# Letting one fill follow another inside a request, and putting the exact heads' outputs behind the exponential

## The chip, the cores and the metric

The kernel runs on one core of one Trainium2 chip. The metric is the device time of one execution in microseconds (us); a run of the comparison gives the median of several executions. TensorE is called PE, VectorE DVE, ScalarE ACT and GpSimd POOL, as in the profile. SyncE (SP) issues nearly all DMAs. PSUM has eight banks of 128 x 512 fp32; here they are one tile, `whole_psum`, cut into views.

## The reference

Three stages follow each other (two batches, eight heads, 576 rows, head size 64; 1152 rows of 512 columns afterwards):

```python
def _attn_ref(q, k, v, tau):
    scores = q @ k.T / sqrt(64)
    thresh = max(scores, -1) - tau
    scores = where(scores >= thresh, scores, -1e9) - max
    attn = exp(scores);  attn = attn / (sum(attn) + 1e-9)
    return attn @ v                              # (2, 8, 576, 64) -> x (1152, 512)

def _moe_ref(x, w_gate, w1, w2):                 # 8 experts, hidden 1024
    P = exp(x @ w_gate - max);  8 times: normalise P over rows, then over columns, times N / E
    return sum_e P[:, e] * (relu(x @ w1[e]) @ w2[e])

def _moe2_ref(x, domain_probs, w1, w2):          # 4 experts
    return sum_e p[:, e] * (relu(x @ w1[e]) @ w2[e])
```

## The kernel before

**Numbers in two parts.** Most matmuls work on fp32r operands, and a value is kept as a high part (a cast by ACT) and a low part (the value less its high part, by POOL or DVE). A product is three matmuls: low times high, high times low, high times high.

**Attention, in steps.** The work is 72 units of 128 query rows. Units 0 to 15 are the first 256 rows of batch 0 (two units for each of eight heads): the *exact heads*, whose probabilities and values are multiplied in fp32 (line 376). Heads 0 and 1 also have fp32 scores (`ws`, line 275), and their exponential has a bias of its own, `st[:, 1:2]`. Units 16 to 35 are the other 320 rows of batch 0 (five units for a pair of heads), units 36 to 71 are batch 1 (nine units for a pair). `Attention.step` is called for t = -2 to 76 and writes out by hand the order in which instructions reach the engines' queues. In step t it handles several units at once: scores of unit t+2 on PE (`scores`), the row maximum of unit t+1 on DVE (`top`, line 287) and its exponential on ACT (`exp`, lines 303 and 305), the mask and row sum of unit t (`mask`, line 309), its reciprocal (`norm`, line 317) and the scaling on POOL (line 319), the five transposes of unit t-2 on PE (`turn`, lines 327 and 329), which have one PSUM bank for all units, their copies out of PSUM (`hi` on ACT, line 341; `lo` on DVE, lines 356 and 358), and the products with V of the head that ended with unit t-3, t-4 or t-5 (`mix`). So the reduction of line 287 with number t+2 belongs to step t.

An exact head's product with V is spread over three steps, so its output comes in step t with unit t-5, in even steps from 6 to 20. `out` puts two things down: on ACT the high part `xh` (line 393), and in a list `later` the low part `xl` on DVE (line 396), which also gives the PSUM bank back. `later` is run in the same step, after the scores of unit t+2. In the order of ACT's queue the output's cast stands ahead of the exponential of unit t+1; the exponential stands ahead of `cook`'s cast of a weight tile (line 107, even steps 0 to 12), whose low part is POOL's (line 109).

**The fill.** Two experts of the first mixture are computed on PE between these steps, by generators (`expert_fill`). Layer 1 is eight hidden tiles of 12 matmuls (line 536), layer 2 one output tile for each 128 rows with 24 matmuls of 512 columns (line 564). A generator yields after four matmuls of layer 1 and after two of layer 2; the yielded number is zero where a tile ends and its bank goes back. `todo` holds four generators with the step after which each may start: expert 0 on rows 0 to 255 (after step 20), expert 0 on rows 256 to 575, expert 1 on rows 0 to 255, expert 1 on rows 256 to 575 (all after step 39). A step calls `fill` twice, ahead of the scores and at the end; both ask `pull(n)` for pieces: three together in a step before step 33, two or one to step 39, four after that, where the second call gets something only with a tile open or with no product with V about. `pull` returns where a tile ends and where a generator ends.

**After the attention** two more generators (expert 1 on batch 1) are put on the list, and a loop runs `pull(3)` until it is empty. The loop's counter n also times the gate (`gate`, from n = 7 on with every third n), the sums of x that the later stages need (`sums`), the scaling of the first two experts (`scale`, lines 933 and 935) and the preparation of weights (`tick`, three times from n = 18). What is left of these goes on in the first part of the next stage.

**The rest**, from 322 us on, are the other experts by a seven-product scheme (lines 1132 and 1444); the diff doesn't touch it.

Of the kernel before, what the change touches and what calls it, by code (L numbers as in the profile page):

```python
# [12 lines left out]
ALU = mybir.AluOpType  # L13
# [14 lines left out]

@with_exitstack
def attention_two_moe_kernel(ctx, tc, qP, kP, qT, kT, vp, tau, wg, w1, w1s, w2, w2s, dp, m2w1s, m2w2, m2w2s, out):  # L30
    nc = tc.nc
    V, A, G, T = nc.vector, nc.scalar, nc.gpsimd, nc.tensor

    def f(ap):
        return ap.bitcast(F32)
# [22 lines left out]
    lin = cp.tile([P, 2], F32, name="lin")  # L58
# [19 lines left out]
    def split(eh, el, hi, lo, src):  # L78
        if eh is A:
            A.copy(hi, src)  # L80
        elif eh is V:
            V.tensor_copy(hi, src)
        else:
            G.tensor_scalar(hi, src, 1.0, 1.0, op0=ALU.mult, op1=ALU.mult)
        el.tensor_tensor(lo, src, f(hi), op=ALU.subtract)  # L85
# [28 lines left out]
    class Expert:  # L114


        def __init__(self, i):
            self.w1 = lambda ft: cooked[2 * FT * i + ft]
            self.w2 = lambda ft: cooked[2 * FT * i + FT + ft]


    class Attention:
# [5 lines left out]
        def __init__(self, pl, ps_s, ps_t, ps_r, ps_m):  # L128
            self.pl, self.ps_s, self.ps_t, self.ps_r, self.ps_m = pl, ps_s, ps_t, ps_r, ps_m
            self.units, self.heads = [], []  # L130
            self.t = -2
            self.work = {}
            self.later, self.late = [], []
            self.iq = self.iv = self.lq = self.lv = 0
            self.xf = {}
            self.e2, self.eth = pl.tile([P, 5, 640], F32, tag="eth", name="e2"), None
            self.e32 = pl.tile([P, 5, 512], F32, tag="etl", name="e32")
            self.etl = None
            self.qz = [pl.tile([P, 3 * D], F32R, name=f"qz{i}") for i in range(2)]
            for z in self.qz:  # L140
                V.tensor_scalar(z[:, D:2 * D], ident[:, :D], 0.0, None, op0=ALU.mult)
# [147 lines left out]
        def line(self, u):  # L289
            st = u["st"]  # L290
            if not u["q"][0][0]["exact"]:
                A.activation(st[:, 2:3], st[:, 0:1], AF.Identity, bias=on[:, 1:2], scale=-1.0)
                return
            if not u["q"][0][0]["ws"]:
                V.tensor_scalar(st[:, 2:3], st[:, 0:1], -1.0, on[:, 0:1], op0=ALU.mult, op1=ALU.subtract)
                return
            V.tensor_scalar(st[:, 1:2], st[:, 0:1], lin[:, 0:1], None, op0=ALU.mult)
            V.tensor_scalar(st[:, 2:3], st[:, 0:1], lin[:, 1:2], None, op0=ALU.subtract)

        def exp(self, u):  # L300
            ex = u["ex"] = self.pl.tile([P, 2, HS], F32, tag="ex", name="ex", bufs=4)
# [85 lines left out]
        def out(self, g):  # L387
            hd, n, pv, pl = g["head"], g["n"], g["pv"], self.pl
            h, t0 = hd["h"], hd["b"] * S + g["q0"]
            r0 = (h % 2) * D  # L390
            r, kt, c = slice(r0, r0 + D), h // 2, slice(t0, t0 + n)
            if hd["exact"]:
                A.copy(xh[r, kt, c], pv[r, :n])

                def low():
                    V.tensor_tensor(xl[r, kt, c], pv[r, :n], f(xh[r, kt, c]), op=ALU.subtract)
                    self.ps_m.give(pv)

                self.later.append(low)
                return  # L400

            key = hd["h"] // 2, g["n"]
            if key not in self.xf:
                self.xf[key] = pl.tile([P, n], F32, tag=f"xf{n}", name="xf", bufs=1)
            xf = self.xf[key]
            o = slice(D - r0, 2 * D - r0)
            A.copy(xf[r, :n], pv[o, :n])

            def rest():
                V.tensor_tensor(xf[r, :n], pv[r, :n], xf[r, :n], op=ALU.add)  # L410
                self.ps_m.give(pv)
                if "half" in self.xf.setdefault(key + ("n",), {}):
                    del self.xf[key], self.xf[key + ("n",)]
                    self.late.append(lambda: split(A, G, xh[:, kt, c], xl[:, kt, c], xf[:, :n]))
                else:
                    self.xf[key + ("n",)]["half"] = True

            self.later.append(rest)
# [5 lines left out]
                w()  # L424

        def flush(self):
            self.run(self.later)
            self.run(self.late)

        def step(self, fill, side):  # L430

            us, t = self.units, self.t
            un = lambda i: us[i] if 0 <= i < len(us) else None
            self.load()
            nxt, a, d, x, c, z, y = (un(t + i) for i in (2, 1, 0, -2, -3, -4, -5))
            if x:
                self.turn(x)
            if d:
                self.mask(d)
            if a:  # L440
                self.top(a)
            if d:
                self.guard(d)
            if a and a["q"][0][0]["exact"]:
                self.line(a)
            if d:
                self.norm(d)
            for part, u in ((2, y), (1, z), (0, c)):
                for g in u["mix"] if u else ():
                    if g["head"]["exact"]:  # L450
                        self.mix(g, part)
            end = t > len(us)
            if x and not end:
                self.hi(x)
            for u, late in ((z, False), (y, True)):
                for g in u["mix"] if u else ():
                    if late == g["head"]["exact"]:
                        self.out(g)
            if end:
                self.run(self.later)  # L460
            if x and end:
                self.hi(x)
            if a:
                self.exp(a)
                if not a["q"][0][0]["exact"]:
                    self.line(a)
            fill(0, bool(c and c["mix"]))
            if x:
                self.lo(x)
            if nxt:  # L470
                self.scores(nxt)
            self.run(self.later)
            for g in c["mix"] if c else ():
                if not g["head"]["exact"]:
                    self.mix(g, 0)
            for w in self.work.pop(t, ()):
                w()
            fill(1, bool(c and c["mix"] or z and z["mix"]))
            self.run(self.late)
            side()  # L480
            self.t += 1
            return self.t < len(us) + 5
# [111 lines left out]
    with ExitStack() as att:  # L594
# [5 lines left out]
        at = Attention(ap, ps_s, ps_t, ps_r, ps)  # L600
# [20 lines left out]
        def side():  # L621
            if at.t >= -1:
                fetch(2)
            if at.t >= nA0 - 3 and raws and room[0] and (at.t % 3 < 2 if at.t < nA1 else room[0] > 2 or at.t % 2):
                room[0] -= 1
                cook()
            if at.t == 20:
                nc.sync.dma_start(wg_sb, wg)
                nc.sync.dma_start(dp_sb, dp)
            if at.t == 24:  # L630
                split(V, V, wg2[:, :, :E1], wg2[:, :, E1:], wg_sb)

        def free(n):
# [4 lines left out]
        todo = [(nA0 + 4, expert_fill(hp, X0, 0, 256, near, acc, None, 0, at.later, keep)),  # L638
                (nA1 + 3, expert_fill(hp, X0, 256, 320, far, acc, tail0[0], 0, at.later, free)),
                (nA1 + 3, expert_fill(hp, X1, 0, 256, near, y1, None, 0, at.later, keep)),  # L640
                (nA1 + 3, expert_fill(hp, X1, 256, 320, far, y1, tail0[1], 0, at.later, keep))]

        left, spent = [0], [0]
        few = dict(zip(range(nA1 - 3, nA1 + 4), (2, 2, 2, 2, 2, 1, 1)))

        def pull(n, end=True):

            for i in range(n):
                if not todo or at.t <= todo[0][0] or (left[0] == 1 and not end):
                    return i  # L650
                left[0] = next(todo[0][1], -1)
                if left[0] < 0:
                    todo.pop(0)
                if left[0] <= 0:
                    left[0] = 0
                    return i + 1
            return n

        def fill(phase, busy):
            if phase == 0:  # L660
                if 0 <= at.t < nA0 - 3 and at.t % 2 == 0:
                    room[0] -= 1
                    cook()
                spent[0] = pull(few.get(at.t, 3))
            elif left[0] or not busy:
                pull(max(few.get(at.t, RA1 if at.t < nA1 + 3 else RA2) - spent[0], 0), True)
# [4 lines left out]
        while left[0]:  # L671
            pull(1)
# [921 lines left out]
```

## Time and profile before

| | us |
|---|---|
| median of 3 runs | 1287.18 (1287.1 to 1287.38) |
| profiled execution, its own time | 1286.37 |
| its span, first to last instruction | 1284.6 |
| PE busy | 1267.8 (99%) |
| POOL, DVE, ACT busy | 897.7 (70%), 880.5 (69%), 736.4 (57%) |

The span is the time from the first to the last instruction; 1.77 us lie around it. An engine's busy time is the union of its instructions. The matmuls' ends are modelled, so a busy PE may still be waiting a little: the distance of two starts is firmer than an idle time. "idle before <- releaser" names the instruction after which an engine could go on.

### The profile page before, as it was taken

The numbers are of one execution on the slowest core, as the hardware profiler recorded it, in microseconds if no ns is written. First come the engines' busy times: TensorE is split into PE (matmuls) and PEld (weight loads), VectorE is DVE, ScalarE is ACT, GpSimd is POOL, SyncE is SP. The second block draws the span as 40 slices with busy tenths as digits, with TensorE's granted clock in tenths as the row PEclk, the third lists the DMA queues.
The fourth block names the chain that finished last, engine by engine and source line by source line (L and its number), as shares of the span: only waits on it lengthen the run. The fifth ranks groups of instructions, "written<-read, shape, count | busy, mean of one in ns | idle before, by whom it ended". The sixth has DMA issues, their size and how long they took to land.

```text
span 1284.6 us, 25109 instructions
## 1 busy us (share of the span) xinstructions
PE 1267.8 (99%) x9373; PEld 1207.6 (94%) x9373; DVE 880.5 (69%) x1851; ACT 736.4 (57%) x1483; POOL 897.7 (70%) x987
## 2 busy tenths in 40 slices
PE   8998999999999999999999999999999999999998
PEld 5597988888889999999999999999989999999998
DVE  6888888666637666666666666666745666666667
ACT  6887887423446555555655555566546465555553
POOL 7997987405796767867776786777668568677770
PEclk9999999999999999999999999999999999999999
DMA  5542330101221112211111221111212012111102
GB/s 171 161 125 78 97 98 17 42 1 34 79 70 51 42 42 58 58 34 51 50 42 42 58 59 34 50 51 42 58 36 61 20 51 58 35 58 50 42 18 74
DMA packets 43225, 73.84 MB, mean 57 GB/s; under 512 B 5216, under 2 KB 12512, under 8 KB 43104
## 3 DMA queue, kind: packets, MB, share of 16 engines
q1 hardware_dynamic: 42816, 71.96, 19.4%
q8 instruction: 74, 1.21, 0.4%
q14 instruction: 47, 0.39, 0.1%
q10 hardware_dynamic: 288, 0.28, 0.1%
HBM read 69.86 MB, written 2.36 MB: 56 GB/s over the span
## 4 chain that ended last, share of the span: by engine, by line
PE 87%; DVE 5%; POOL 3%; issue 2%; ACT 2%; DMA 0%; SPq 0%; DVEq 0%; POOLq 0%; ACTq 0%
PE mm L1132 34%; PE mm L1444 33%; PE mm L564 5%; PE mm L536 5%; PE mm L282 2%; PE mm L1252 2%; PE mm L327 2%; DVE ex L309 1%; PE mm L376 1%; POOL wl L85 1%; DVE st L287 1%; PE mm L385 1%; DVE etl L358 1%; PE mm L383 1%; ACT ex L305 1%
## 5 line engine op out<-in xcount | busy, mean ns | idle before, releaser
L85 POOL TENSOR_TENSOR wl<-raw,wh 128x512 fp32r<-128x512 f32 x217 | 282.9, 1310 | 179.8 <-ACT wh L80 166.6
L1232 DVE SCALAR_TENSOR_TENSOR acc<-mm,p,acc 128x256 f32<-128x256 f32 (+1 forms) x428 | 195.3, 508 | 72.2 <-PE mm L1444 59.3
L1444 PE MATMUL mm<-wh,h 128*128 128x256 f32 x960 | 173.3, 279 | 0.0
L1139 ACT COPY snap<-mm 128x576 f32<-128x576 f32 x126 | 80.9, 642 | 157.1 <-DVE mm L1293 77.9
L80 ACT CAST wh<-raw 128x512 fp32r<-128x512 f32 x217 | 133.5, 627 | 47.3 <-PE mm L1444 26.4
L1444 PEld LDWEIGHTS mm<-wh,h 128*128 128x128 f32 x960 | 146.5, 188 | 0.0
L1132 PE MATMUL mm<-xh,wl 128*128 128x288 f32 x672 | 145.7, 298 | 0.3
L1132 PE MATMUL mm<-xh,wh 128*128 128x288 f32 x672 | 143.3, 294 | 0.0
L1132 PE MATMUL mm<-xl,wh 128*128 128x288 f32 x672 | 143.0, 294 | 0.0
L1444 PE MATMUL mm<-wl,h 128*128 128x256 f32 x480 | 134.5, 280 | 0.1
L1444 PE MATMUL mm<-wh,tails 128*128 128x256 f32 x696 | 126.1, 279 | 0.0
L85 POOL TENSOR_TENSOR wl<-sum,wh 128x512 fp32r<-128x512 f32 x82 | 107.1, 1307 | 8.2 <-ACT wh L80 8.1
L1132 PEld LDWEIGHTS mm<-xh,wl 128*128 128x128 f32 x672 | 106.3, 188 | 3.1 <-DVE mm L1152 0.5
L1132 PE MATMUL mm<-xth,wl 128*128 128x288 f32 x504 | 108.1, 295 | 0.1
L1132 PE MATMUL mm<-xtl,wh 128*128 128x288 f32 x504 | 107.7, 294 | 0.0
L1132 PE MATMUL mm<-xth,wh 128*128 128x288 f32 x504 | 107.5, 294 | 0.0
L1132 PEld LDWEIGHTS mm<-xl,wh 128*128 128x128 f32 x672 | 107.5, 188 | 0.0
L1132 PEld LDWEIGHTS mm<-xh,wh 128*128 128x128 f32 x672 | 107.3, 188 | 0.0
L1444 PEld LDWEIGHTS mm<-wh,tails 128*128 128x128 f32 x696 | 106.2, 188 | 0.0
L80 ACT CAST wh<-sum 128x512 fp32r<-128x512 f32 x82 | 51.5, 628 | 85.4 <-POOL sum L829 71.9
L1444 PE MATMUL mm<-wl,tails 128*128 128x256 f32 x348 | 97.2, 279 | 0.0
L1444 PEld LDWEIGHTS mm<-wl,h 128*128 128x128 f32 x480 | 90.1, 188 | 0.5 <-issue 0.3
(242 smaller groups left out, 3487.8 us busy)
## 6 DMA issues: line engine op xcount, KB each, us to landing
raw<-in_w1s SPq DMA_DIRECT2D x56, 256.0 KB, 2.6
raw<-in_w2s SPq DMA_DIRECT2D x48, 256.0 KB, 2.6
raw<-in_w SPq DMA_DIRECT2D x40, 256.0 KB, 3.2
raw<-in_m2w1s SPq DMA_DIRECT2D x32, 256.0 KB, 2.6
raw<-in_m2w2s SPq DMA_DIRECT2D x28, 256.0 KB, 2.7
kr<-in_kT SPq DMA_DIRECT2D x22, 288.0 KB, 3.0
vr<-in_vp SPq DMA_DIRECT2D x24, 160.0 KB, 2.3
qr<-in_qT SPq DMA_DIRECT2D x8, 288.0 KB, 2.9
```

The lines of the kernel that those rows point to most:

```text
L80: A.copy(hi, src)
L85: el.tensor_tensor(lo, src, f(hi), op=ALU.subtract)
L282: T.matmul(sc[:m, hf, :HS], lhsT=q, rhs=kk[:, hf * HS:(hf + 1) * HS], start=i == 0, stop=i == len(ops) - 1)
L287: V.tensor_reduce(st[:, 0:1], u["sc"][:, :, :HS], axis=AX.XY, op=ALU.max, negate=not u["q"][0][0]["ws"])
L327: T.transpose(et[:, kt], exf[:, kt * P:(kt + 1) * P], ident)
L536: T.matmul(ph[:, :n], lhsT=a[:, kt * P:(kt + 1) * P], rhs=x[:, kt, n0:n0 + n], start=i == 0 and kt == 0, stop=i == 2 and kt == KT - 1)
L564: T.matmul(py, lhsT=x, rhs=a, start=i == 0, stop=i == 3 * FT - 1)
L1132: T.matmul(ch[b][:, g, :HS], lhsT=w[:, (2 * g + kt) * P:(2 * g + kt + 1) * P], rhs=operand(u, kt, lo), start=first and j == 0, stop=j == l ...
L1139: A.copy(v[u], m)
L1232: V.scalar_tensor_tensor(a, src, s, a, op0=ALU.mult, op1=ALU.add)
L1252: T.matmul(py, lhsT=hid[x][:, kk, o:o + P], rhs=w[y], start=n == 0, stop=n == 3 * HF - 1)
L1444: T.matmul(m, lhsT=hid(x, kt + ko), rhs=wk[y], start=first and n == 0, stop=n == 5, skip_group_check=True)
```

## The change

The diff does four things. (1) `pull` goes on with the next generator where one ends, within the same request, instead of returning. (2) In an exact head's output step the exponential of unit t+1 and the cast of a weight come ahead of the output's cast `xh`. (3) The output's low part goes to a list `behind`, which is run in the next step, after the reciprocal and ahead of the products with V. (4) On DVE the bias of heads 0 and 1 is made right after the maximum, and the reciprocal comes ahead of the threshold's instruction (`line`).

```diff
@@ -130,7 +130,7 @@
             self.units, self.heads = [], []
             self.t = -2
             self.work = {}
-            self.later, self.late = [], []
+            self.later, self.late, self.behind = [], [], []
             self.iq = self.iv = self.lq = self.lv = 0
             self.xf = {}
             self.e2, self.eth = pl.tile([P, 5, 640], F32, tag="eth", name="e2"), None
@@ -294,8 +294,11 @@
             if not u["q"][0][0]["ws"]:
                 V.tensor_scalar(st[:, 2:3], st[:, 0:1], -1.0, on[:, 0:1], op0=ALU.mult, op1=ALU.subtract)
                 return
+            V.tensor_scalar(st[:, 2:3], st[:, 0:1], lin[:, 1:2], None, op0=ALU.subtract)
+
+        def bias(self, u):
+            st = u["st"]
             V.tensor_scalar(st[:, 1:2], st[:, 0:1], lin[:, 0:1], None, op0=ALU.mult)
-            V.tensor_scalar(st[:, 2:3], st[:, 0:1], lin[:, 1:2], None, op0=ALU.subtract)
 
         def exp(self, u):
             ex = u["ex"] = self.pl.tile([P, 2, HS], F32, tag="ex", name="ex", bufs=4)
@@ -396,7 +399,7 @@
                     V.tensor_tensor(xl[r, kt, c], pv[r, :n], f(xh[r, kt, c]), op=ALU.subtract)
                     self.ps_m.give(pv)
 
-                self.later.append(low)
+                self.behind.append(low)
                 return
 
             key = hd["h"] // 2, g["n"]
@@ -424,6 +427,7 @@
                 w()
 
         def flush(self):
+            self.run(self.behind)
             self.run(self.later)
             self.run(self.late)
 
@@ -439,12 +443,14 @@
                 self.mask(d)
             if a:
                 self.top(a)
+            if a and a["q"][0][0]["ws"]:
+                self.bias(a)
             if d:
                 self.guard(d)
+                self.norm(d)
             if a and a["q"][0][0]["exact"]:
                 self.line(a)
-            if d:
-                self.norm(d)
+            self.run(self.behind)
             for part, u in ((2, y), (1, z), (0, c)):
                 for g in u["mix"] if u else ():
                     if g["head"]["exact"]:
@@ -452,19 +458,21 @@
             end = t > len(us)
             if x and not end:
                 self.hi(x)
-            for u, late in ((z, False), (y, True)):
-                for g in u["mix"] if u else ():
-                    if late == g["head"]["exact"]:
-                        self.out(g)
+            for g in z["mix"] if z else ():
+                if not g["head"]["exact"]:
+                    self.out(g)
             if end:
                 self.run(self.later)
             if x and end:
                 self.hi(x)
             if a:
                 self.exp(a)
-                if not a["q"][0][0]["exact"]:
-                    self.line(a)
+            if a and not a["q"][0][0]["exact"]:
+                self.line(a)
             fill(0, bool(c and c["mix"]))
+            for g in y["mix"] if y else ():
+                if g["head"]["exact"]:
+                    self.out(g)
             if x:
                 self.lo(x)
             if nxt:
@@ -646,11 +654,14 @@
         def pull(n, end=True):
 
             for i in range(n):
-                if not todo or at.t <= todo[0][0] or (left[0] == 1 and not end):
-                    return i
-                left[0] = next(todo[0][1], -1)
-                if left[0] < 0:
-                    todo.pop(0)
+                left[0] = -1
+                while left[0] < 0:
+                    if not todo or at.t <= todo[0][0]:
+                        left[0] = 0
+                        return i
+                    left[0] = next(todo[0][1], -1)
+                    if left[0] < 0:
+                        todo.pop(0)
                 if left[0] <= 0:
                     left[0] = 0
                     return i + 1
```

## Rows read from the trace of the kernel before

**Rows 1.** The page's head and its first part: busy us (share) and instructions.

```profile
span 1284.6 us, 25109 instructions
...
PE 1267.8 (99%) x9373; PEld 1207.6 (94%) x9373; DVE 880.5 (69%) x1851; ACT 736.4 (57%) x1483; POOL 897.7 (70%) x987
```

**Rows 2.** Windows of PE's stages: us, busy time of each engine (instructions), clock, DMA.

```profile
20.00:60.00 40.00, 39.61 (x213) 24.06 (x211) 32.27 (x102) 34.26 (x68) 37.46 (x43) 1.00 0.51 149
60.00:132.00 72.00, 66.97 (x459) 59.69 (x458) 64.60 (x165) 58.02 (x131) 59.96 (x72) 1.00 0.36 103
132.00:232.00 100.00, 98.40 (x684) 91.45 (x683) 86.64 (x222) 78.69 (x176) 80.38 (x115) 1.00 0.24 68
232.00:322.00 90.00, 90.00 (x544) 79.79 (x543) 54.49 (x150) 26.15 (x65) 31.04 (x78) 1.00 0.08 27
```

**Rows 3.** PE's waits over the span: us in total, times, longest.

```profile
PE mm L327 <- DVE etl L358: 2.7, 6, 0.9
```

**Rows 4.** Line 287: duration min/median/max in ns, first and last start in us.

```profile
L287 DVE TENSOR_REDUCE st<-mm x72: 744/753/758, 6.0 to 227.9; 128x1 f32<-128x576 f32 x72
```

**Rows 5.** Timeline, steps 0 and 1: start, us, engine, line, what [idle before].

```profile
9.37 0.14 DVE L313 TENSOR_SCALAR st<-st 128x1 f32<-128x1 f32 x1
...
9.80 0.83 ACT L303 ACTIVATE ex<-mm,st,esc 128x576 f32<-128x576 f32 x1 [0.47 <-DVE st L297]
```

**Rows 6.** Timeline of ACT and POOL around an exact output (step 8).

```profile
30.15 0.37 ACT L393 CAST xh<-mm 64x256 fp32r<-64x256 f32 x1 [0.67 <-PE mm L376]
30.55 0.74 ACT L305 ACTIVATE ex<-mm,st 128x576 f32<-128x576 f32 x1
...
31.18 0.61 ACT L107 CAST wh<-raw 128x512 fp32r<-128x512 f32 x1
...
31.88 1.27 POOL L109 TENSOR_TENSOR wl<-raw,wh 128x512 fp32r<-128x512 f32 x1 [0.31 <-ACT wh L107]
```

**Rows 7.** POOL's waits from 12 to 44 us.

```profile
POOL wl L109 <- ACT wh L107: 1.6, 4, 0.7
```

**Rows 8.** Timeline, the transposes of step 16.

```profile
49.75 0.66 PE L327 MATMUL mm<-ident,ex 128*128 128x128 f32 x4 [0.18 <-POOL ex L319]
```

**Rows 9.** Timeline of DVE and PE, steps 20 and 21.

```profile
64.45 0.43 DVE L396 TENSOR_TENSOR xl<-mm,xh 64x256 fp32r<-64x256 f32 x1
...
64.93 0.82 DVE L309 SCALAR_TENSOR_TENSOR ex<-mm,st,ex 128x576 f32<-128x576 f32 x1
...
65.07 0.62 PE L536 MATMUL mm<-xl,wh 128*128 128x256 f32 x4
...
66.60 0.67 DVE L358 TENSOR_TENSOR tails<-mm,eth 128x512 fp32r<-128x512 f32 x1
```

**Rows 10.** Timeline, steps 39 and 40.

```profile
126.47 0.27 PE L329 MATMUL mm<-ident,ex 128*64 128x128 f32 x1
...
127.70 0.88 POOL L85 TENSOR_TENSOR xl<-xf,xh 128x320 fp32r<-128x320 f32 x1 [1.94 <-ACT xh L80]
...
127.77 0.53 PE L282 MATMUL mm<-kh,qs 128*128 128x288 f32 x2 [1.03 <-DVE ex L309]
```

**Rows 11.** The chain that ended last, from 128 us: start, us, what.

```profile
130.17 1.76 PE mm L536 x12
```

**Rows 12.** Timeline, steps 55 and 56.

```profile
178.16 0.59 ACT L568 COPY acc<-mm 128x512 f32<-128x512 f32 x1 [1.23 <-PE mm L564]
...
180.11 0.63 PE L327 MATMUL mm<-ident,ex 128*128 128x128 f32 x4 [0.91 <-DVE etl L358]
```

**Rows 13.** Timeline of PE in step 71.

```profile
229.64 0.63 PE L327 MATMUL mm<-ident,ex 128*128 128x128 f32 x4 [0.16 <-DVE etl L358]
```

**Rows 14.** Lines 933 and 935: as rows 4.

```profile
L933 DVE TENSOR_SCALAR acc<-acc,p x9: 479/481/491, 308.6 to 322.8; 128x512 f32<-128x512 f32 x9
...
L935 DVE SCALAR_TENSOR_TENSOR acc<-y,p,acc x4: 750/753/754, 312.5 to 316.1; 128x512 f32<-128x512 f32 x4
```

**Rows 15.** Timeline of DVE at the start of the next stage.

```profile
328.80 0.76 DVE L1141 TENSOR_TENSOR mm<-snap,mm 128x576 f32<-128x576 f32 x1 [3.32 <-PE mm L1132]
```

## The prediction

> **What bounds the kernel now.** Read the page's first part first: PE is busy 1267.8 of 1284.6 us [rows 1]. Then cut the span by stage: from 232 us on PE is full (90.00 of 90), so whatever happens there, its matmuls set the time; from 20 to 60 us it is nearly full (39.61 of 40), from 60 to 132 us it lacks 5.03 us, from 132 to 232 us 1.60 us [rows 2]. So the change can give back only PE's idle time in the attention, and the fill's matmuls are the same before and after: one that runs earlier in a hole shortens the loop behind the attention by its own length, one that runs earlier where PE is full shortens nothing. PE's waits say who makes the holes: mostly the transposes, whose one PSUM bank is emptied late by DVE [rows 3]. Steps are found in the trace by line 287, whose 72 reductions are the steps -1 to 70 [rows 4].
>
> **The handover.** Going through `fill` and `pull` with the counts of the code (units of 2 for an exact head, 5 and 9 for a pair): the first generator's last piece falls in step 39. Before, steps 40, 55 and 70 ask for three pieces and get nothing, since the first request meets a generator's end, and the second call is refused there (no tile open, a product with V about). After, step 40 already does the second generator's first tile, and everything behind comes forward: the third generator begins in step 54 instead of 56, the fourth in 68 instead of 71. In the loop the ends of generators cost nothing any more, and 24 matmuls of layer 2 have gone into the attention: 41 requests instead of 48. Each of the three steps is one hole:
>
> Step 40. PE ends its transposes and waits 1.03 us for the mask before the scores [rows 10]. The new tile is 12 matmuls of 320 columns, 1.76 us [rows 11], and stands just there. But it needs rows 256 to 575 of every head, and the last head's low part is POOL's only from 127.70 to 128.58 [rows 10]. The eighth matmul, the last that multiplies it, can't start before; after it five of 0.147 us remain (1.76 / 12), so the scores start at about 129.3 instead of 127.77. 1.5 to 1.6 us later for 1.76 us of work: a gain of 0.2 us. It is bounded by the whole wait, 1.03, and by -0.3, if DVE's row maximum (which has to wait for these scores) is late by some tenths.
>
> Step 55. PE waits 0.91 us for its next transposes, since ACT copies an output tile out at 178.16 ahead of the copy that empties the transposes' bank [rows 12]. After, that output ends in step 53, and PE has a tile of layer 1 in step 54 and another in 55 to do meanwhile. I take the whole 0.9. The ends are 0 (the wait turns up before another of the fill's tiles) and 0.91.
>
> Step 70. 0.16 us of waiting at the transposes behind it [rows 13]; I take 0.15, between 0 and 0.16.
>
> Sum 1.25, at most 2.1, at least -0.5. On the same three holes the Trainium skill has a rule ("Perfetto Trace Analysis", section "Per-instruction lifecycle: what the profiler-reported window actually captures"): a matmul's end in a profile is computed from its size, not observed, so an idle time behind one is no measurement. By it the hole of step 40 is better taken between starts, 126.47 to 127.77 [rows 10], an upper end of 1.30 instead of 1.03; with that the sum's upper end would be 2.4. No run here shows the end itself; the view's 1.03 is 127.77 less 126.47 less the modelled 0.27.
>
> What comes forward with it: weights of expert 1 are cooked as its predecessor's tiles come free, one of them in step 44 instead of 48 (a cast on ACT and a low part on POOL, 0.61 and 1.27 us as in [rows 6], and SP's fetch for the next); neither engine is full there, and I count nothing for it. In the loop, the gate keeps its beat of three requests and ends at request 39 of 41, not of 48: three scaled tiles (of nine; two of 0.48 + 0.75 us, one of 0.48, together 2.9 us [rows 14]) go behind the loop, into DVE's queue in the next stage. DVE idles 3.32 us there before line 1141 [rows 15], so they are hidden, with little to spare: 0 to 0.3 us, I take 0. PE has no hole in the loop that the missing requests could open (90.00 of 90 [rows 2]).
>
> **The exact heads.** Heads 0 and 1: the exponential waits for its bias, and the bias for `guard`, 0.14 us [rows 5]. The guard goes behind it. PE's scores there wait for the mask, so the first steps gain 0.14 us once (0 to 0.42 over three steps).
>
> Output steps: ACT waits 0.67 us for the product with V, casts the output (0.37 us), and only then starts the exponential, at 30.55; the weight's cast comes after it, and POOL has waited 0.31 us for that [rows 6]; 1.6 us of such waits lie between 12 and 44 us [rows 7]. After, exponential and cast start some 0.5 us earlier. But PE is what is full in these steps: all that it can win from 20 to 60 us is 40 - 39.61 = 0.39 us [rows 2], of which the one place that POOL holds up is 0.18 us [rows 8]. I take 0.2, between 0 and 0.39. The output's cast, now behind the weight's, and its low part, now a step later on DVE, hold only the PSUM bank of that product; the next one but one that needs it comes in the step behind that, after the low part in DVE's and PE's order. On DVE the low part's 0.43 us move from the end of an even step to the middle of an odd one, ahead of the copies that free the transposes' bank; the earlier exponential (0.37 us of cast that it no longer waits for) pays for it. No moved instruction issues a DMA, and SP's queue keeps its order.
>
> The last output is the exception. It comes in step 20, and step 21 begins the fill, whose tile needs rows 0 to 255 of all heads: the eighth matmul multiplies the last head's low part. Before, that is made at 64.45 to 64.88, at the end of step 20, and the four matmuls that use it start at 65.07, and span 0.62 us, so that the eighth starts about 0.35 later, at 65.4 [rows 9]: just in time. After, it stands in step 21 behind mask, maximum, guard and reciprocal. From the mask's start to the next thing behind the reciprocal is 66.60 - 64.93 = 1.67 us [rows 9]. The mask itself can come earlier by about 0.45 us (0.43 of low part and 0.37 of cast are no longer ahead of it), so the low part is there at 64.93 - 0.45 + 1.67 + 0.43 = 66.58 instead of 64.88. PE's fill waits 66.58 - 65.4 = 1.18 us, and behind the waiting matmul stand in PE's queue five more of the tile, the scores of unit 23, a product with V and the next transposes; ACT's copies and its next exponential wait for those. I take 1.1 us. The ends: 0, if PE arrives that much later for other reasons or later holes swallow it, and 1.6, if the mask gains nothing.
>
> Sum for the exact heads: -0.14 - 0.2 + 1.1 = +0.8 us; with -1.25 from the handover, -0.45 us. The profiled execution took 1286.37 us, 1.77 more than its span; less 0.45 that is 1285.92. The median is 0.81 us above this execution, so **1286.7 us** is what I predict for it.
>
> **Rivals.** (a) The handover is worth its holes whole and step 21 costs nothing: PE's later holes (5.03 us to 132 us [rows 2]) take the delay in. For it: most of PE's waits for DVE at the transposes [rows 3] come after step 21; against: DVE waits in its turn for what PE is late with. -0.14 - 0.39 - 2.1 = -2.6: 1284.6 us.
>
> (b) Slower: the wait of the fill in step 21. Its place is the eighth matmul of line 536, its price is the time from 65.4 to the end of the low part, at most 1.6 us (mask not earlier), and it decides as soon as it is more than the handover and the first steps give together. The handover gives nothing if the tile in step 40 waits as reckoned and the hole of step 55 only moves by two steps; then 1287.18 + 1.6 = 1288.8 us. For it: all of the chain that it stands in (low part, matmul, scores, transposes) is visible in one step; against: the exponential's earlier start, which pays part.
>
> (c) The change doesn't do what it says: the three empty steps are filled, but where PE was held by DVE it is held a step later, and step 21 costs what the rest gives: 1287.2 us.
>
> **Chances.** The forecast 0.45, (a) 0.25, (b) 0.15, (c) 0.15. No change is here what a measurement of this kernel can't tell from it, 0.2% or 2.6 us either way: below 1284.6 lie most of (a), 0.2, and 0.05 of the forecast's own spread; above 1289.8 lie half of (b), whose price could add to other new waits, and 0.02 more; so faster 0.25, same 0.65, slower 0.10. The range goes from 1284.1, a little below (a), to 1288.7, all but the end of (b).
>
> **What would show it.** In the trace after: requests for the fill in steps 40, 54, 55 and 70 with PE's wait for the mask in step 40 turned into one for POOL's `xl` inside line 536; no wait of 0.9 us at the transposes near 180 us; the exponential of even steps starting right behind DVE's maximum; the weights' low parts on POOL without waits between 23 and 44 us; PE's wait of about 1.1 us inside the first fill tile near 65 us, released by DVE line 396; PE as full from 232 us on as now. The forecast is wrong if no such wait stands in step 21, if the hole of step 55 is still there under another name, or if the next stage begins with PE waiting for DVE.

## The result, and the profile after

The changed kernel takes 1300.12 us (median of 5 runs, 1299.61 to 1300.39) against 1287.26 us of the kernel before (5 runs, 1287.1 to 1287.4): a ratio of 1.0099, 95% interval 1.0087 to 1.011. It is 12.9 us slower; 1286.7 us was predicted. In the changed kernel's lines the numbers have moved by 3 to 11: 327, 358, 396 and 568 are now 330, 361, 399 and 576; 536, 564, 933 and 1132 are 544, 572, 944 and 1143; line 919 is the gate's matmul, line 916 the last of the DVE instructions in front of it, and line 85 makes low parts everywhere.

The page's head and its first part answer to [rows 1]; PE has 5.4 us more of busy time for the same 9373 matmuls:

```profile
span 1298.4 us, 25098 instructions
...
PE 1273.2 (98%) x9373; PEld 1212.6 (93%) x9373; DVE 883.1 (68%) x1851; ACT 736.2 (57%) x1483; POOL 898.0 (69%) x987
```

The windows by stage (columns as in [rows 2]: us, busy time of each engine, granted clock, DMA) show where:

```profile
20.00:60.00 40.00, 39.73 (x213) 24.21 (x213) 33.32 (x104) 34.61 (x68) 37.81 (x43) 1.00 0.53 150
60.00:132.00 72.00, 66.33 (x451) 58.82 (x450) 62.91 (x158) 56.50 (x127) 58.45 (x74) 1.00 0.37 103
132.00:232.00 100.00, 98.60 (x685) 91.90 (x684) 84.05 (x216) 77.83 (x173) 79.93 (x115) 1.00 0.23 68
...
308.00:312.00 4.00, 0.92 (x6) 0.43 (x4) 2.38 (x10) 1.93 (x5) 4.00 (x10) 1.00 0.35 90
312.00:316.00 4.00, 4.00 (x12) 3.18 (x12) 3.62 (x11) 0.00 (x0) 3.29 (x11) 0.57 0.36 109
316.00:328.00 12.00, 12.00 (x55) 9.84 (x54) 4.17 (x18) 3.69 (x9) 1.31 (x1) 1.00 0.00 0
328.00:332.00 4.00, 2.02 (x15) 1.77 (x13) 3.72 (x7) 1.68 (x3) 0.98 (x1) 1.00 0.26 66
332.00:336.00 4.00, 1.56 (x6) 1.48 (x7) 4.00 (x7) 0.00 (x0) 2.07 (x2) 0.59 0.40 116
336.00:340.00 4.00, 4.00 (x20) 4.00 (x20) 2.92 (x6) 1.16 (x2) 1.39 (x1) 0.56 0.06 19
```

The attention is about as full as before. Behind it, where PE had 90.00 of 90 us, there are two holes, and behind each hole a stretch in which PE is busy all the time while the granted clock is at half for most of it (0.57 and 0.56 over 4 us): from 312.05 to 315.46 us the matmuls start 0.43 us apart, from 315.78 us on 0.23 us. PE's waits over the whole span (us, times, longest) name the two, and the new small ones of the attention:

```profile
PE mm L1143 <- DVE xtl L85: 4.4, 1, 4.4
...
PE mm L919 <- DVE p L916: 3.1, 1, 3.1
PE mm L330 <- DVE etl L361: 2.6, 6, 0.8
...
PE mm L544 <- DVE xl L399: 1.1, 1, 1.1
...
PE mm L572 <- POOL wl L109: 0.9, 1, 0.9
PE mm L544 <- ACT acc L576: 0.6, 1, 0.6
```

**The first hole**, timeline of the changed kernel, last generator's layer 1 (ACT, then DVE, then PE). ACT's queue is in order: the cast of a weight's `sum` waits 3.72 us for POOL, the hidden tile's `hh` stands behind it, DVE's `hl` waits for that, the gate's eight small instructions stand behind `hl`, and PE's next gate matmul waits for the last of them:

```profile
308.39 0.62 ACT L80 CAST wh<-sum 128x512 fp32r<-128x512 f32 x1 [3.72 <-POOL sum L840]
308.92 0.76 ACT L550 ACTIVATE hh<-mm 128x320 fp32r<-128x320 f32 x2
...
309.38 0.49 DVE L553 SCALAR_TENSOR_TENSOR hl<-mm,hh 128x320 fp32r<-128x320 f32 x1 [3.41 <-ACT hh L550]
309.79 0.23 DVE L920 TENSOR_REDUCE mm<-mm 128x8 f32<-128x72 f32 x1
...
311.80 0.44 PE L919 MATMUL mm<-p,ones 128*128 128x72 f32 x2 [3.08 <-DVE p L916]
```

**The second hole**, DVE and PE where the next stage begins. Between the copy of the last output tile and the six low parts `xtl` that the stage's first units need (the *splits* below; the expectations call them Strassen splits, after the seven-product scheme) stand the scalings of four tiles (four of line 944, two of line 946); in the kernel before one stood there. (A view's group of line 944 counts three of them as one row.)

```profile
328.21 0.69 DVE L576 COPY acc<-mm 128x512 f32<-128x512 f32 x1 [2.87 <-PE mm L572]
328.82 1.27 DVE L944 TENSOR_SCALAR acc<-acc,p 128x512 f32<-128x512 f32 x3
...
331.31 1.64 DVE L946 SCALAR_TENSOR_TENSOR acc<-y,p,acc 128x512 f32<-128x512 f32 x1
332.87 3.35 DVE L85 TENSOR_TENSOR xtl<-sums,xth 128x288 fp32r<-128x288 f32 x6
...
334.44 0.98 PE L1143 MATMUL mm<-xtl,wh 128*128 128x288 f32 x2 [4.42 <-DVE xtl L85]
```

About 2 us of this wait is slower work and not more of it: POOL makes low parts of weights from 331.02 to 334.06 us, and beside it the last scaling took 1.64 us where the others of line 946 took 0.75, and the first `xtl` 1.51 us where the other five took 0.45.

The account: waits of 3.08 and 4.42 us; half clock, as the missing share of the clock times its stretch, 0.43 x 4 = 1.7 us behind the first, 0.41 x 1.56 (from 334.44) + 0.44 x 4 = 2.4 us behind the second; the exact heads 0.85 us (below); a start 0.26 us later (the first scores at 3.92 instead of 3.66 us). That is 12.7 of the 13.8 us between the spans. The sixty-first matmul of the next stage's line comes 12.88 us later than before, so 0.9 us more lie behind it, and nothing in the traces names them. The medians lie 12.86 us apart: the profiled execution of the kernel before took 1286.37 us, 0.9 less than the median beside the changed kernel, so these 0.9 us may be no more than the spread of executions.

### The profile page after: what moved, and what is told of

Its sections match the earlier page's. It is cut to its first block, busy times and chain, and to the rows that moved or that the text cites. A ratio compares the mean times of both kernels' runs of the same rounds, so it can differ in the third digit from the quotient of the medians.

```text
span 1298.4 us, 25098 instructions
## 1 busy us (share of the span) xinstructions
PE 1273.2 (98%) x9373; PEld 1212.6 (93%) x9373; DVE 883.1 (68%) x1851; ACT 736.2 (57%) x1483; POOL 898.0 (69%) x987
## 4 chain that ended last, share of the span: by engine, by line
PE 87%; DVE 6%; ACT 3%; POOL 2%; issue 1%; DMA 0%; DVEq 0%; ACTq 0%; POOLq 0%
PE mm L1143 36%; PE mm L1455 33%; PE mm L572 4%; PE mm L544 3%; PE mm L1263 3%; PE mm L282 2%; DVE ex L312 2%; PE mm L330 1%; PE mm L379 1%; DVE st L287 1%; PE mm L388 1%; ACT ex L308 1%; POOL wl L85 1%; PE mm L386 1%; DVE hl L553 1%
```

## The experiments

Theory T: the loop behind the attention is a timetable counted in requests (weights from request 18, a step of the gate at every third, scaling once the gate is over), and the handover shortened PE's work under it by seven requests, 48 to 41. The weights then meet the last generator's layer 1 (requests 21 to 28, before 28 to 35), and the scaling, which before had ten requests (39 to 48), has three (39 to 41). Rivals: R1, the exact heads' new order; R2, the work moved into the attention and its new waits; R3, PE's clock falling by itself. Every median stands beside the kernel before on the same chip.

**The two parts apart.** e1 is the changed kernel with `pull` of before, e2 the kernel before with the new `pull`.

> The exact heads' new order alone, with the pull of before. Theory T (the loss is made in the loop behind the attention, whose 48 requests the handover cuts to 41): 1288.1 us, that is 1287.26 + 0.8 from the wait in step 21 (1.15 us at the eighth fill matmul), with no wait of PE over 1 us between 246 and 334 us and a full granted clock there. Rival R1 (the reorder sets the 13 us): about 1300 us.

> The handover alone, exact heads as before. T: 1299.3 us (1300.12 less 0.8), with the waits of about 3.1 us behind the gate's DVE chain and 4.4 us in front of the Strassen splits still there. R1: about 1287 us. Rival R2 (the loss is made inside the attention by the moved fill work and its new waits): also near 1299, but with the first gate matmul later than 255.1 less 0.8 less 0.3 = 254.0 us.

e1: 1287.85 against 1287.2 us, ratio 1.0006 (0.9997 to 1.0014); the loop is as full as before. e2: 1299.16, ratio 1.0096 (1.0082 to 1.011), with waits of 3.1 and 4.4 us at the same two places. R1 falls. The first matmul of the gate is at 254.21 us in e2, 254.94 in the changed kernel, 246.5 before. That is 0.2 us past the mark set for R2, far less than the loss, so e2 alone doesn't decide on R2.

**Where the handover counts.** A switch in `pull` lets it hand over in one place only: `if not hand[0]: break` where a generator ends, with `hand` true in the attention alone (e7) or in the loop alone (e12).

> The kernel before with the handover inside the attention alone; in the loop a finished part still ends its request. The loop then has 43 requests, its gate ends at 39, eight of nine tiles can be scaled by request 43, and the last generator's layer 1 stands at requests 23 to 30 beside the weight preparation at 20 to 27. T: part of both waits, between 1288 and 1297 us, nearest 1293; the first gate matmul as late as with the whole handover (about 254 us). Rival R2 (the moved work in the attention itself sets the loss): 1299.

> The kernel before with the handover in the loop alone: 46 requests, the last generator's layer 1 at requests 26 to 33, the weight preparation at 20 to 27 touches only its first two, and all nine tiles are scaled by the end of the loop. T: both waits small or none: 1287 to 1288.5 us. R2: 1287.

e7: 1293.55 against 1286.73, 1.0052 (1.0039 to 1.0064): the wait at the splits is 4.2 us, the one at the gate 0.3. The first gate matmul is at 253.99, as late as in e2, yet the loss is 6.8 us instead of 12.0: R2 can't be the whole cause. e12: 1288.22 against 1287.32, 1.0005 (0.9996 to 1.0014), no wait over 0.2 us in the loop. The dose fits T: 46 requests cost nothing measurable, 43 cost the second hole, 41 both.

**The timetable alone.** Two runs move the timetable of the kernel before and leave the handover out. e9:

```diff
-        if n >= 18:
+        if n >= 25:
...
-        if n < 7 or n % 3 == 0 and gated:
+        if n < 7 or n % 3 == 1 and gated:
...
-        elif not gated and l1[0] >= FT:
+        elif not gated and l1[0] >= FT and n >= 46:
```

> The kernel before, with no handover and the exact heads as before; only the loop's timetable is moved as seven requests fewer would move it: weight preparation from request 25 (not 18), gate at requests that leave 1 by 3 (not 0), scaling not ahead of request 46. Theory T (the timetable against the work is the whole loss): the two waits of PE appear without the change, about 3 us at the gate in the last generator's layer 1 and about 4.4 us at the splits, with half clock behind each: 1286.9 + 3.1 + 1.7 + 4.4 + 2.7, or 1298.8 us, 1297 to 1301. Rival R2 (the work moved into the attention is needed for the loss): 1287.

1293.95 against 1287.32, 1.0051 (1.0038 to 1.0063): the wait at the splits is there, 4.4 us, the one at the gate is not. The trace says why. ACT's hold is there too (ACT and DVE of e9):

```profile
306.32 0.62 ACT L80 CAST wh<-sum 128x512 fp32r<-128x512 f32 x1 [2.98 <-POOL sum L829]
...
307.31 0.49 DVE L545 SCALAR_TENSOR_TENSOR hl<-mm,hh 128x320 fp32r<-128x320 f32 x1 [3.45 <-ACT hh L542]
...
308.70 0.20 DVE L915 TENSOR_REDUCE mm<-dp_sb 128x9 f32<-128x36 f32 x1
```

but my edit had let the gate begin two requests early against the work, so that its last matmul ran at 303.23 us: behind the held `hl` stood only the gate's tail on DVE, for which PE doesn't wait. e13 shifts without that fault: seven requests of the loop pass with no step of the timetable.

```diff
+        if n == 6 and idle:
+            idle -= 1
+            continue
         n += 1
```

> The kernel before, with no handover and the exact heads as before; in the loop seven requests for fill work pass without a step of the timetable (no gate, no sums, no weights, no scaling), behind the sixth. From there on the timetable stands against the work as in the changed kernel: the last generator's layer 1 at its requests 21 to 28, the end at 41. Theory T: both waits come, 3.1 us at the gate and 4.4 us at the splits, each with half clock behind it: 1287.2 plus 12, or 1299 us. If the gate's wait needs the moved work: 1294, with the wait at the splits alone.

1297.54 against 1286.99 us, 1.0087 (1.0073 to 1.0101): both waits come in the kernel before, at the same operations and of the same length (PE's waits of e13; then its windows behind the first and the second):

```profile
PE mm L1136 <- DVE xtl L85: 4.4, 1, 4.4
...
PE mm L908 <- DVE p L905: 3.1, 1, 3.1
```

```profile
312.00:316.00 4.00, 4.00 (x11) 3.12 (x10) 2.83 (x9) 0.00 (x0) 2.50 (x9) 0.50 0.19 60
...
336.00:340.00 4.00, 4.00 (x19) 4.00 (x18) 3.13 (x7) 1.16 (x2) 1.18 (x1) 0.50 0.10 35
```

So 10.6 us of e2's 12.0 come with no work moved into the attention; the other 1.4 us are not explained. (The profiled execution of e13 took 1299.96 us, with 0.994 of the clock; the three others 1297.2 to 1297.6 us, with 0.997.)

**Taking the causes away one by one.** e3 prepares the weights from request 12 (`if n >= 12`).

> The changed kernel with the weight preparation started at the 12th request of the loop, not the 18th, so that its casts lie beside the layer 2 of the generator before and not beside the last generator's layer 1. T: the 3.1 us wait of PE on the gate goes, and with it the stretch at half clock behind it (about 1.75 us): 1295.1 us; the 4.4 us wait in front of the next stage stays. Rival R3 (the clock falls by itself, not because of the wait): 1297, with a granted clock under 0.9 somewhere in 300 to 320 us. If the gate's own chain is the limit and not the casts ahead of it: 1300, wait unchanged.

1294.73 against 1287.2, 1.006 (1.0046 to 1.0074); the changed kernel less 5.4. The gate's wait is 0.4 us, and the clock stays full there; R3 falls, for the half clock went with the wait. The wait at the splits is 4.4 as before. e4 takes the scaling out of the loop:

```diff
-            for _ in range(2):
-                next(sl, None)
+            pass
```

> The changed kernel with no scaling of the output tiles in the loop: all nine go behind the next stage's work. T: the 4.4 us wait for the splits and the half clock behind it (about 2.7 us) go, less up to 1 us for seven microseconds more of DVE work in the next stage: 1292.8 to 1293.8 us; the 3.1 us wait stays. Rival: the splits wait for the sums themselves (the last part of the Strassen sums), and not for the scaling: 1300 with the wait still over 3 us.

A miss: 1301.95 against 1287.2, 1.0114 (1.0101 to 1.0128). The splits come right behind the copy now, as T said (first row, DVE of e4), but the scalings follow them ahead of the next stage's combinations (the third row is the first of them), and PE waits 7.7 us for the second (`PE mm L1142 <- DVE mm L1162`):

```profile
330.08 2.29 DVE L85 TENSOR_TENSOR xtl<-sums,xth 128x288 fp32r<-128x288 f32 x6
332.29 7.33 DVE L944 TENSOR_SCALAR acc<-acc,p 128x512 f32<-128x512 f32 x5
...
342.86 0.76 DVE L1151 TENSOR_TENSOR mm<-snap,mm 128x576 f32<-128x576 f32 x1
```

All nine are 9 x 0.48 + 4 x 0.75 or 7.3 us of DVE [rows 14], and in order they fit neither in front of the splits nor right behind them; the place that is left is beside PE's layer 2. And five scalings take 7.33 us, 1.5 each, where one took 0.48 [rows 14]: POOL works on weights in the same stretch. e6 makes that place, with a step of the gate at every second request, so that the scaling starts at request 33:

```diff
-        if n < 7 or n % 3 == 0 and gated:
+        if n < 7 or n % 2 == 0 and gated:
```

> The gate at every second request alone, weight preparation from the 18th as in the changed kernel. T: the wait in front of the splits and its half clock go (7.1 us), the gate's wait behind the casts of the sums stays or splits over two gate steps: 1292 to 1294 us. If the two waits hang together: 1287 or 1300.

> The changed kernel with the weight preparation from the 12th request and a step of the gate at every second request of the loop (not every third), so that the gate ends at request 28 and the scaling stands at requests 33 to 41, beside the last generator's layer 2. Theory T: both waits of PE (3.1 and 4.4 us) and both stretches at half clock go: 1294.7 less 4.4 less 2.7, or 1287.6 us, though the loop has 41 requests as in the changed kernel. Rival (with seven requests fewer the work no longer fits beside PE, wherever it is put): above 1291 us, with a wait of over 2 us somewhere between 255 and 345 us.

e6: 1289.01 against 1286.73, 1.0018 (1.0009 to 1.0027), 41 requests and no wait at the splits; better than expected, since the gate's wait fell to 0.6 us too; that its steps now meet other requests of layer 1 is the likely reason, which no run isolates. e5, with the weights from request 12 besides: 1292.46, 1.0044 (1.0032 to 1.0057), a miss in the other direction. The early weights have moved ACT's hold to the beginning of layer 1; DVE's sums come late behind it and take 1.39 and 1.55 us beside POOL, and a gate step now stands behind them (ACT, DVE and PE of e5):

```profile
295.27 0.62 ACT L80 CAST wh<-sum 128x512 fp32r<-128x512 f32 x1 [2.56 <-POOL sum L840]
...
297.98 1.55 DVE L971 TENSOR_TENSOR extra<-sums,extra 128x288 f32<-128x288 f32 x1
...
301.85 0.69 PE L919 MATMUL mm<-p,ones 128*128 128x72 f32 x2 [2.57 <-DVE p L916]
```

**A better version?** e11 is e6 with two small holes of the attention mended, e8 the same on e5, e10 the same with the weights from request 8:

```diff
-                self.behind.append(low)
+                (self.later if self.t == 20 else self.behind).append(low)
...
-            if at.t >= nA0 - 3 and raws and room[0] and (at.t % 3 < 2 if at.t < nA1 else room[0] > 2 or at.t % 2):
+            if at.t >= nA0 - 3 and raws and room[0] and (at.t % 3 < 2 if at.t < nA1 else True):
```

> The kernel of the gate at every second request and early weights, with two more edits: the last exact head's low part in its own step again (takes the 1.15 us wait of step 21 away), and a weight tile of the fill prepared at every step of the last stage (takes the 0.9 us wait for an expert's weight in step 64 away). T: 1287.6 less 1.0 less 0.9, or 1285.7 us, below both kernels by 0.1%. If POOL's queue takes the extra casts badly: 1287 to 1289.

> The changed kernel with the gate at every second request, the last exact head's low part in its own step, a weight tile prepared at every step of the last stage, and the weight preparation from request 8, so that it is over (request 17) before the last generator's layer 1 begins (request 21). T: the 2.6 us wait at the gate that the same kernel had with the preparation from request 12 goes, with its half clock: 1290.7 less 2.6 less 1.5, or 1286.6 us, and no wait of PE over 0.6 us from 232 to 345 us. If the gate itself at every second request is too fast for the layer 1 beside it: still over 1289.

> The same with the weight preparation from request 18, as in the changed kernel: 1289.0 less 1.0 (the wait of step 21) less 0.9 (the wait for the expert's weight in step 64), or 1287.1 us, with a wait of about 0.6 us at the gate.

e8: 1290.72 against 1286.73, 1.0029 (1.0017 to 1.0041): 1.7 us below e5, as the two mends promised, but with e5's wait of 2.6 us at the gate. e10: 1289.62 against 1287.32, 1.0017 (1.0009 to 1.0026): two waits at the gate, together 2.1 us, at 284 and 288 us, now because the gate's chain shares DVE with sums that take up to 1.45 us instead of 0.45 while POOL prepares weights. e11: 1287.8, 1.0004 (0.9995 to 1.0013): the best with the handover, and no better than the kernel before.

**The exact heads alone, mended** (the first of those two edits on e1):

> The exact heads' new order alone, but the low part of the last one (step 20) in its own step again. T: the 1.15 us wait of PE in step 21 is gone and the exact part's cost with it: 1287.2 less 0.3, or 1286.9 us, against 1287.85 for the exact part as it is. If the wait was covered by something else that now ends last: 1287.9.

1286.88 against 1286.99, 1.0 (0.9991 to 1.0009); the wait of step 21 is gone from the list. It lies 1.0 us below e1, as the wait's length says, though the two come from different comparisons, and each interval is wider than that. No version here beats the kernel before by what can be measured.

## Why the prediction was wrong

**The step that failed** is the last of the handover: "PE has no hole in the loop that the missing requests could open (90.00 of 90 [rows 2])", and with it the three scaled tiles "hidden, with little to spare: 0 to 0.3 us, I take 0". The first was worth 3.08 + 1.7, the second 4.42 + 2.4 us. A full PE before says nothing of what DVE and ACT will do once PE comes earlier. I had counted the seven requests and where the gate ends, but not which operation of the timetable then stands beside which work: that the weights start at request 18 whatever the fill does is in the code, and the hold was in the trace of before. There it fell on the first three tiles of layer 1 and cost PE nothing: DVE was at a gate step until 295.33 us in any case, so `hl` lost 0.29 us, and the first gate matmul that depends on what stands behind it ran at 301.20 us (ACT and DVE of the kernel before):

```profile
294.62 0.62 ACT L80 CAST wh<-sum 128x512 fp32r<-128x512 f32 x1 [2.77 <-POOL sum L829]
295.15 1.18 ACT L542 ACTIVATE hh<-mm 128x320 fp32r<-128x320 f32 x3
...
295.62 1.29 DVE L545 SCALAR_TENSOR_TENSOR hl<-mm,hh 128x320 fp32r<-128x320 f32 x3 [0.29 <-ACT hh L542]
```

For the scaling I looked for idle time of DVE behind the loop (3.32 us [rows 15]) and found it in the wrong place: it lies behind the six low parts that PE waits for, and the scalings stand ahead of them. Nor was the count right: three tiles are left behind the loop, but of the six scaled in the loop four came in its last two requests, behind the last copy. No rival had this; the one on the slower side stood in step 21, at 1288.8. Only the last of the prediction's signs of being wrong named it: "if the next stage begins with PE waiting for DVE".

**What was right.** Exact heads, predicted +0.8: the reduction of step 39 starts at 124.94 instead of 123.83 us, less 0.26 of the later start is +0.85, and e1's median says +0.65. The low part of the last head is there at 66.37 (66.58 predicted, [rows 9] of before), and the eighth matmul of the tile waits 1.15 us (1.18 predicted; part of that closeness is luck, since the low part came 0.2 us and PE 0.1 us earlier than reckoned):

```profile
65.94 0.43 DVE L399 TENSOR_TENSOR xl<-mm,xh 64x256 fp32r<-64x256 f32 x1
...
66.42 0.39 PE L544 MATMUL mm<-xl,wh 128*128 128x256 f32 x1 [1.15 <-DVE xl L399]
```

POOL's waits for the weight's cast between 12 and 44 us fell from 1.6 [rows 7] to 1.0 us, and PE is busy 39.73 of 40 us there instead of 39.61.

**Handover in the attention**, predicted -1.25, came out at nothing: the gate's first matmul is 8.43 us later, and of that 12 matmuls of layer 1 at 0.147 and 24 of layer 2 at 0.233 us are 7.36, the exact heads 0.85 and the start 0.26. Without the exact heads, e7 puts the handover there at a loss of 0.1 us and e2 at one of 0.5. (The sum's lower end of -0.5 was itself off: its terms give -0.3.) Step 40 gives 0.1 (scores at 130.56, so 1.7 us behind where they were, for 1.76 us of work); the bank that the tile needs comes 0.57 us late, which I had not reckoned. The 0.9 us of step 55 are gone [rows 12], but 0.9 us stand in step 64: expert 1's weight is cooked in the step ahead of its use, now that its use comes earlier. I had counted "nothing" for those weights. So the term that was mis-sized here is the handover's 1.25.

```profile
128.41 0.85 PE L544 MATMUL mm<-xh,wl 128*128 128x320 f32 x4 [0.57 <-ACT acc L576]
...
130.56 0.43 PE L282 MATMUL mm<-kh,qs 128*128 128x288 f32 x2
...
213.79 0.51 PE L572 MATMUL mm<-wl,hh 128*128 128x512 f32 x1 [0.90 <-POOL wl L109]
```

## What to carry to other kernels

Where one engine's progress is the clock for the others' work (a counter of requests), shortening its work is a change of the timetable: list for every counted event what it stands beside before and after, and what is queued behind it in order. A full engine is full because its feeders arrive in time, so look, queue by queue, at how much they have to spare at the new place. And an idle time counts as cover only if it lies ahead of what the critical engine waits for.

## What was not expected of the hardware

**The clock's price.** PE's granted clock stayed at 1.00 through the waits of 0.9 and 1.1 us (the changed kernel, e10), and was at half (0.50, the 1.2 GHz level) in the stretch behind waits of 2.6 (e5), 3.1, 4.4 and 7.7 us (e4); each time it came back to 1.00 while PE was busy. In the changed kernel that adds 1.7 us to a wait of 3.1 and 2.4 us to one of 4.4: more than half as much again. The wait alone doesn't set the price. Behind the same wait of 3.1 us, the time from that gate matmul to the next, with 18 matmuls of layer 2 between them, was 6.06 us in the changed kernel, 7.10 in e13 and 7.38 in e4, against 4.42 at full clock; what makes the difference is not shown.

**DVE beside POOL.** Scaling a tile took 0.48 us in all nine cases of the kernel before and 1.51 to 1.58 us in five of e4, each beside POOL's work for nine tenths of its time or more; a sum of 128x288 took 0.45 us alone, up to 1.56 beside POOL. The Trainium skill ("SBUF — State Buffer", section "SBUF: two separate sides") says that the two share a pair of ports as an exclusive lock for a whole instruction, not as split bandwidth; of DVE's instructions this concerns those with two inputs in SBUF or in a two-port mode. The durations agree with it, not with a constant slowdown: some sums beside POOL still took 0.46 us. No run here shows the lock itself.
